# One-token attention decode on one core: all heads but the last summed in one full-width PSUM bank, then carried by an fp32 product into four column groups

## The chip, the cores and the metric

One core of a Trainium2 chip. The time is the device time of one launch, in microseconds. The profile is one execution taken by the hardware profiler; its span (188.0 us) is about 1.8 us shorter than the time reported for the same execution. PE is TensorE, DVE is VectorE, ACT is ScalarE, POOL is GpSimd, SP is the engine that issues the transfers.

## The reference, cut to what matters

```python
x  = A_x                                  # 2 x 1 x 448
xn = layernorm(x)
# attention: 16 query heads on 8 key heads of width 256,
# over the last 4096 positions of two caches
q = xn @ wq
p = softmax(q k^T / 16)
attention = concat_heads(p v) @ wo        # wo: 4096 x 448
dense = mish(xn @ w1 + b1) @ w2           # w2: 1792 x 448
out = x + attention + dense               # 2 x 448
```

The last key window and value window are 4 MB each per key head. All of the output is one sum over contraction blocks of 128 rows: 1 block for x, 14 for the dense part, 4 for each of the 8 key heads.

## The kernel before

The sum lives in PSUM, split into four column groups of 112 of the 448 output columns, each on its own 32 PSUM partitions, so that four matmuls run side by side in the array (16 of them took 0.37 us at 149 us):

```python
NO = NQ                      # 4
DO = D // NO                 # 112
psA = [ps_a.tile([P, DO], FP32, name=f"psA{u}") for u in range(2)]

def part(n):
    return psA[n // 2][n * Q : n * Q + Bsz, :]

def add(lhsT, w, start=False, stop=False):
    for n in range(NO):
        nc.tensor.matmul(part(n), lhsT=lhsT, rhs=w[:, n*DO:(n+1)*DO],
                         start=start, stop=stop, tile_position=(0, n * Q), ...)
```

The loop over key heads is a pipeline: step i scores head i, computes the values of head i-1 and closes head i-2. For the last two heads the values are computed with the cache as the stationary operand, 128 matmuls of 4 columns each:

```python
def values_fixed(i):                       # heads 6 and 7
    state["rec", i] = denominator(i)       # one fp32 matmul, one DVE reciprocal
    ...
    for t in range(T):                     # T = 64
        for c in range(ND):                # ND = 2
            nc.tensor.matmul(po[:, c, :], lhsT=vv[:, t, c, :], rhs=pTv[:, th, 0:Q:HS], ...)
    scale_o(i, po)                         # DVE, writes oT

def mix(kvh):                              # "output matmuls" below: 4 calls of add
    ...
    for h in range(rep):
        for c in range(ND):
            add(oT[:, c, h, :], w[:, h, c * D : (c + 1) * D], stop=...)

for i in range(Hkv + 1):
    ...
    # in step 8, in this order: mix(6), values_fixed(7), scale, mix(7)
```

Head 7's V block arrives in three pieces (positions 0 to 31, 32 to 55, 56 to 63 of 64), so that its values can begin early. The last call of the kernel, `issue_in_order`, makes every engine issue in program order.

The softmax here doesn't subtract the row's maximum and nothing guards it: scores larger than these inputs give would overflow.

Of the kernel before, what the change touches and what calls it, by code (L numbers as in the profile page):

```python
# [12 lines left out]
FP32 = mybir.dt.float32  # L13
# [21 lines left out]
def kernel(  # L35
# [13 lines left out]
    nc = tc.nc  # L49
    P = 128  # L50
    Q = 32
    NQ = P // Q

    Bsz, Sq, D = A_x.shape
    _, Hkv, Sk, Dh = A_k_cache.shape
    HqDh = A_wq.shape[1]
    Hq = HqDh // Dh
    rep = Hq // Hkv
# [14 lines left out]
    ND = Dh // P  # L73
# [9 lines left out]
    ident = lead.tile([P, P], BF16)  # L83
# [5 lines left out]
    consts = ctx.enter_context(tc.tile_pool(name="consts", bufs=1))  # L89
# [5 lines left out]
    ps_a = ctx.enter_context(tc.tile_pool(name="ps_a", bufs=1, space=PSUM))  # L95
# [3 lines left out]
    x_bf = consts.tile([Bsz, D], BF16)  # L99
# [13 lines left out]
    for lo, hi in ((0, SC), (SC, NS)):  # L113
# [4 lines left out]
    ident_f = consts.tile([Q, Q], FP32)  # L118
# [11 lines left out]
        out=rstd[:], in_=mv[:, 1:2], func=ACT.Sqrt, bias=eps_t[:], scale=1.0  # L130
# [5 lines left out]
    for r in range(2):  # L136
        n = (NS + 1 - r) // 2
        nc.vector.tensor_scalar(  # L138
            out=xn_bf[:, r : NS : 2, :, :],
# [12 lines left out]
    for j in range(1, NQ):  # L152
        nc.vector.tensor_tensor(
            out=hsel, in0=hsel, in1=ident[:, j * Q : (j + 1) * Q : HS], op=ALU.add
# [4 lines left out]
    for b in range(Bsz):  # L159
        nc.vector.tensor_reduce(  # L160
            out=off[:, b : b + 1], in_=hsel[:, b * rep : (b + 1) * rep], axis=AXIS.X, op=ALU.add
# [4 lines left out]
        out=off[:], in0=off[:], scalar1=mine[:], scalar2=1e4, op0=ALU.subtract, op1=ALU.mult  # L166
# [12 lines left out]
    for s in range(NS):  # L179
# [7 lines left out]
        out=odd[:],  # L187
        in_=ident[:].rearrange("p (u o) -> p o u", o=2),
# [4 lines left out]
    for par in range(2):  # L193
        for x in range(NX):
            which = (par + x) % 2
            nc.vector.tensor_scalar(
                out=xs[:, par : NS : 2, x, :],
# [6 lines left out]
    nc.vector.memset(ones[:], 1.0)  # L204



    NO = NQ
    DO = D // NO
    psA = [ps_a.tile([P, DO], FP32, name=f"psA{u}") for u in range(2)]  # L210

    def part(n):
        return psA[n // 2][n * Q : n * Q + Bsz, :]

    def add(lhsT, w, start=False, stop=False):
        for n in range(NO):
            nc.tensor.matmul(  # L217
                part(n),
                lhsT=lhsT,
                rhs=w[:, n * DO : (n + 1) * DO],  # L220
                start=start,
                stop=stop,
                tile_position=(0, n * Q),
                skip_group_check=True,
            )

    add(ident[0:Bsz, 0:Bsz], x_bf[:, :], start=True)


    xq = consts.tile([P, NS, NQ, Q], BF16)  # L230
# [102 lines left out]
    def dense_out():  # L333
        w2_sb = dense.pop("w2")
        for x in range(NX):
            for c in range(NF):
                add(act_bf[:, c, x, :], w2_sb[:, x, c, :])
# [13 lines left out]
    def load_k(i, cuts=(0, T)):  # L351
        k_t[i] = k_pool.tile([P, T * Dh], BF16, tag="k", name="k")
        load_cache(k_t[i], A_k_cache, i, cuts)

    def load_v(i, cuts=(0, T)):
        t = v_tile()
        load_cache(t, A_v_cache, i, cuts)
        v_t[i] = t[:].rearrange("p (t d) -> p t d", t=T)

    def load_wo(kvh, parts=1):  # L360
        w = wo_pool.tile([P, rep, ND * D], BF16, tag="wo", name="wo")
        r0 = kvh * rep * Dh
        win = A_wo[r0 : r0 + rep * Dh, :].rearrange("(h p c) d -> p h (c d)", h=rep, p=P)
        for u in range(parts):
            hs = slice(u * rep // parts, (u + 1) * rep // parts)
            nc.sync.dma_start(out=w[:, hs, :], in_=win[:, hs, :])
        wo_t[kvh] = w

    def turn(s):
        kt = kt_pool.tile([P, TH * Dh], BF16, tag="kt", name="kt")  # L370
        i, half = divmod(s, NH)
        k = k_t[i] if half < NH - 1 else k_t.pop(i)
        nc.vector.transpose(  # L373
            out=kt[:].bitcast(FP32),
            in_=k[:, half * TH * Dh : (half + 1) * TH * Dh].bitcast(FP32),
        )
        kt_t[s] = kt

    def scores(s):
        i = s // NH  # L380
        ktv = kt_t.pop(s)[:].rearrange("p (t n c e) -> p n e t c", t=TH, n=NB, e=NE)
        psc = ps_sc.tile([P, TH, Q], FP32, tag="sc", name="sc")
        for n in range(NB):
            for e in range(NE):
                nc.tensor.matmul(  # L385
                    psc[:],
                    lhsT=qdiag[i % NW][:, n * NE + e, :],
                    rhs=ktv[:, n, e, :, :],
                    start=(n == 0 and e == 0),
                    stop=(n == NB - 1 and e == NE - 1),  # L390
                )
        p_sb = p_pool.tile([P, TH * Q], BF16, tag="p", name="p")
        piece = s % NH
        if piece == 0:
            state["rs", i] = small.tile([P, NH, Bsz], FP32, tag="rs", name="rs")
        pv = p_sb[:].rearrange("p (t c b) -> p b t c", t=TH, b=Bsz)
        sv = psc[:].rearrange("p t (c b) -> p b t c", b=Bsz)
        for b in range(Bsz):
            nc.scalar.activation(  # L399
                out=pv[:, b, :, :],  # L400
                in_=sv[:, b, :, :],
                func=ACT.Exp,
                scale=scale,
                bias=off[:, b : b + 1],
                accum_out=state["rs", i][:, piece, b : b + 1],
            )
        p_t[s] = p_sb

    def turn_p(s):
        pT = p_pool.tile([P, TH * Q], BF16, tag="pT", name="pT", bufs=2 * NH + 1)  # L410
        nc.vector.transpose(out=pT[:], in_=p_t.pop(s)[:])  # L411
        pT_t[s] = pT
        i, half = divmod(s, NH)
        if half != NH - 1:
            return
        rs = state.pop(("rs", i))
        total = small.tile([P, 1], FP32, tag="total", name="total")
        nc.vector.tensor_reduce(out=total[:], in_=rs[:], axis=AXIS.XY, op=ALU.add)
        sums = small.tile([P, BR], FP32, tag="sums", name="sums")
        nc.vector.tensor_scalar(  # L420
            out=sums[:], in0=hsel, scalar1=total[:], scalar2=None, op0=ALU.mult
        )
        state["sums", i] = sums
# [45 lines left out]
    def finish(i):  # L469
        ov = state.pop(("o", i))[:].rearrange("r (u m c) -> r u c m", u=NP, c=ND)  # L470
        pq = ps_q.tile([P, NP * ND * NR], FP32, tag="q", name="q")
        pqv = pq[:].rearrange("p (u c r) -> p u c r", u=NP, c=ND)
        for u in range(NP):
            for c in range(ND):
                nc.tensor.transpose(pqv[:, u, c, :], ov[:, u, c, :], ident_f[0:NR, 0:NR])  # L475
        o = small.tile([P, ND, BR], FP32, tag="osum", name="osum")
        nc.vector.tensor_copy(out=o[:], in_=pqv[:, 0, :, 0:BR])
        for u in range(1, NP):
            nc.vector.tensor_tensor(  # L479
                out=o[:], in0=o[:], in1=pqv[:, u, :, u * BR : (u + 1) * BR], op=ALU.add  # L480
            )
        scale_o(i, o)
# [21 lines left out]
    def mix(kvh):  # L504
        oT = state.pop(("oT", kvh))
        w = wo_t.pop(kvh)
        for h in range(rep):
            for c in range(ND):
                add(
                    oT[:, c, h, :],  # L510
                    w[:, h, c * D : (c + 1) * D],
                    stop=(kvh == Hkv - 1 and h == rep - 1 and c == ND - 1),
                )

    NFIX = 2
# [1 line left out]
    def close(i):  # L517
        if i < Hkv - NFIX:
            finish(i)
        mix(i)  # L520
# [7 lines left out]
    for i in range(Hkv + 1):  # L528
        if i + 1 < Hkv:
            load_k(i + 1, (0, T) if i + 1 < Hkv - 1 else (0, T // 2, T))  # L530
        if i < Hkv:
            load_v(i, (0, T) if i < Hkv - 1 else (0, T // 2, 7 * T // 8, T))
            load_wo(i, parts=1 if i < Hkv - 1 else 2)
            for piece in range(NH):
                s = i * NH + piece
                if s + 1 < NSTEP:
                    turn(s + 1)
                scores(s)
                if s >= 1:
                    turn_p(s - 1)  # L540
                if s == NSTEP - 1:
                    turn_p(s)
                if piece == 0 and i > 1:
                    close(i - 2)
            if i + 2 < Hkv:
                build_q(i + 2)
        else:
            close(i - 2)
        if i == 0:
            dense_in()  # L550
            dense_out()
        if i >= 1:
            if i - 1 < Hkv - NFIX:
                values(i - 1)
            else:
                values_fixed(i - 1)
        if i == Hkv:
            close(i - 1)

    res = consts.tile([Bsz, D], BF16)  # L560
    for n in range(NO):
        copy = nc.vector.tensor_copy if n // 2 == 0 else nc.scalar.copy
        copy(out=res[:, n * DO : (n + 1) * DO], in_=part(n))
# [32 lines left out]
```

## Time and profile before

| | |
|---|---|
| time, median of 3 | 190.17 us (189.82 to 190.40) |
| HBM read | 77.67 MB, 413 GB/s over the span |
| busy share of PE, DVE, ACT | 75%, 57%, 23% |
| second piece of the last V block lands | 182.28 us |
| PE idle ahead of that landing | 1.58 us |
| work after that landing to the store | 3.5 us |

Read it from the right: the span is mostly one long stream of transfers, and the end is that stream plus the few steps behind its last landings. What PE does in the stream is free as long as it is ready by then. One more line of this page also belongs here, which the prediction passed over; it counts the transfers that bring the engines' own instructions (queue, kind: packets, MB, share):

```profile
q8 instruction: 8, 0.13, 0.3%
```

Eight transfers, 0.13 MB: 16 KB each.

### The profile page before, as it was taken

What the parts mean: (1) busy time and instruction counts of PE and PEld (TensorE: products, weight loads), DVE (VectorE), ACT (ScalarE), POOL (GpSimd) and SP (SyncE); (2) the same over time, 40 slices, a digit from 0 to 9 for tenths busy, and PEclk for the clock granted to TensorE, in tenths of its full rate; (3) what the DMA queues carried; (4) which work ended last, traced back from release to release, by engine and by line L of the source; (5) the groups of instructions that cost most, each with busy time, mean ns of one, the idle gap of its engine ahead of it and who ended that gap; (6) DMA issues with size and microseconds to landing.
All of it is one profiled execution on the core that took longest, in us unless ns stands there. A gap on an engine that the chain in (4) does not pass through costs nothing.

```text
span 188.0 us, 2587 instructions
## 1 busy us (share of the span) xinstructions
PE 140.3 (75%) x1030; PEld 67.3 (36%) x1030; DVE 106.6 (57%) x141; ACT 42.5 (23%) x142; POOL 16.4 (9%) x74
## 2 busy tenths in 40 slices
PE   0396098905989779966795599956996699988863
PEld 0132033903434334423341334422442334433762
DVE  6604497049931994089704991099506983967201
ACT  3004015200440315012421224021511233134101
POOL 7000600300020001100030003000020000000000
PEclk9999659955999978999999969997899969999855
DMA  6999899999999999999999999999999999999991
GB/s 220 421 476 439 383 426 439 446 443 446 432 439 436 399 404 435 439 439 394 474 441 439 418 404 429 432 446 413 452 446 422 398 425 422 457 439 411 411 385 38
DMA packets 5653, 77.83 MB, mean 414 GB/s; under 512 B 517, under 2 KB 2569, under 8 KB 2954
## 3 DMA queue, kind: packets, MB, share of 16 engines
q1 hardware_dynamic: 5636, 77.66, 97.0%
q8 instruction: 8, 0.13, 0.3%
q10 hardware_dynamic: 6, 0.01, 0.0%
q14 instruction: 3, 0.02, 0.0%
HBM read 77.67 MB, written 0.00 MB: 413 GB/s over the span
## 4 chain that ended last, share of the span: by engine, by line
DMA 67%; DVE 19%; PE 11%; SPq 1%; ACT 1%; issue 0%; ACTq 0%; DVEq 0%
DMA k<-in_A_k_cache_dram 57%; DVE kt L373 14%; DMA v<-in_A_v_cache_dram 10%; PE sc L385 6%; PE o L444 4%; DVE pT L411 3%; PE q L494 1%; ACT p L399 1%; PE psA L217 1%; SPq L114 0%; DVE oT L458 0%; DVE sums L420 0%; SPq L349 0%; DVE osum L479 0%; ACTq L591 0%
## 5 line engine op out<-in xcount | busy, mean ns | idle before, releaser
L373 DVE STREAM_TRANSPOSE kt<-k 128x2048 f32<-128x2048 f32 x32 | 73.1, 2288 | 54.3 <-DMA k<-in_A_k_cache_dram 54.3
L385 PE MATMUL sc<-kt,qdiag 128*128 128x512 bf16 x256 | 68.1, 421 | 19.1 <-DVE kt L373 18.1
L399 ACT ACTIVATE p<-sc,off 128x256 bf16<-128x256 f32 x64 | 33.0, 545 | 72.8 <-PE sc L385 72.1
L385 PEld LDWEIGHTS <-qdiag 128*128 128x128 bf16 x256 | 25.5, 105 | 59.0 <-issue 27.1
L444 PE MATMUL o<-v,pT 128*8 128x512 bf16 x192 | 42.5, 379 | 0.0
L444 PEld LDWEIGHTS <-pT 128*8 128x8 bf16 x192 | 17.2, 92 | 22.4
L266 POOL COPY qdiag<-qt 32x16 bf16<-32x16 bf16 x64 | 13.0, 248 | 120.7 <-PE sc L385 103.8
L411 DVE STREAM_TRANSPOSE pT<-p 128x512 bf16<-128x512 bf16 x32 | 21.5, 673 | 2.5 <-ACT p L399 2.4
L399 ACT ACTIVATION_READ_ACCUMULATOR p<-sc,off 128x1 f32 x64 | 11.8, 184 | 0.0
L452 ACT COPY o_sb<-o 8x512 f32<-8x512 f32 x6 | 3.5, 575 | 36.3 <-PE o L444 36.3
L217 PE MATMUL psA<-wo,oT 128*2 128x112 bf16 x128 | 3.3, 229 | 9.5 <-DVE oT L458 9.5
L246 PE MATMUL q_ps<-v,xq 128*128 128x512 bf16 x28 | 8.8, 491 | 2.0 <-DVE xq L237 2.0
L494 PE MATMUL q<-pT,v 128*128 128x4 bf16 x256 | 7.4, 168 | 2.1 <-DMA v<-in_A_v_cache_dram 1.6
L494 PEld LDWEIGHTS <-v 128*128 128x128 bf16 x256 | 7.4, 101 | 2.3 <-DMA v<-in_A_v_cache_dram 1.7
L217 PE MATMUL psA<-v,act_bf 128*2 128x112 bf16 x56 | 1.5, 296 | 6.5 <-DVE act_bf L331 6.5
L256 DVE CAST q_sb<-q_ps 128x512 bf16<-128x512 f32 x2 | 1.3, 684 | 8.3 <-PE q_ps L246 8.3
L246 PEld LDWEIGHTS <-xq 128*128 128x128 bf16 x28 | 3.3, 121 | 7.2 <-issue 3.5
L217 PEld LDWEIGHTS <-oT 128*2 128x2 bf16 x128 | 1.7, 84 | 10.2 <-DVE oT L458 10.2
L180 PE MATMUL xnT_ps<-ident,xn_bf 2*128 2x2 bf16 x7 | 0.5, 165 | 5.7 <-DVE xn_bf L138 5.7
L458 DVE TENSOR_TENSOR oT<-q,rec 128x8 bf16<-128x8 f32 x2 | 0.3, 166 | 7.0 <-PE q L494 7.0
L475 PEld LDWEIGHTS q<-ident_f,o_sb 8*128 8x128 f32 x24 | 3.3, 207 | 2.6 <-issue 2.6
L475 PE MATMUL q<-ident_f,o_sb 8*128 8x8 f32 x24 | 3.8, 264 | 0.0
(54 smaller groups left out, 43.4 us busy)
## 6 DMA issues: line engine op xcount, KB each, us to landing
k<-in_A_k_cache_dram SPq DMA_DIRECT2D x7, 4096.0 KB, 29.5
v<-in_A_v_cache_dram SPq DMA_DIRECT2D x7, 4096.0 KB, 29.5
k<-in_A_k_cache_dram SPq DMA_DIRECT2D x2, 2048.0 KB, 24.5
v<-in_B_w_dram SPq DMA_DIRECT2D x2, 1568.0 KB, 24.0
wo<-in_A_wo_dram SPq DMA_DIRECT2D x7, 448.0 KB, 30.1
v<-in_A_wq_dram SPq DMA_DIRECT2D x1, 2048.0 KB, 7.5
v<-in_A_v_cache_dram SPq DMA_DIRECT2D x1, 2048.0 KB, 15.1
v<-in_A_wq_dram SPq DMA_DIRECT2D x1, 1536.0 KB, 10.7
```

The lines of the kernel that those rows point to most:

```text
L217: nc.tensor.matmul(part(n), lhsT=lhsT, rhs=w[:, n * DO : (n + 1) * DO], start=start, stop=stop, tile_position=(0, n * Q), skip_group_check ...
L246: nc.tensor.matmul(ps[u][:], lhsT=xq[:, s, :, :].rearrange("p j k -> p (j k)"), rhs=wq_sb[:, s, u * N5 : (u + 1) * N5], start=(s == 0), st ...
L256: copy(out=q_sb[:, u * N5 : (u + 1) * N5], in_=ps[u][:])
L266: nc.gpsimd.tensor_copy(out=tv[rows, :, e, j * Q : (j + 1) * Q : HS].rearrange("p n (b h) -> p n b h", b=Bsz), in_=qv[rows, :, h0 : h0 + r ...
L373: nc.vector.transpose(out=kt[:].bitcast(FP32), in_=k[:, half * TH * Dh : (half + 1) * TH * Dh].bitcast(FP32),)
L385: nc.tensor.matmul(psc[:], lhsT=qdiag[i % NW][:, n * NE + e, :], rhs=ktv[:, n, e, :, :], start=(n == 0 and e == 0), stop=(n == NB - 1 and ...
L399: nc.scalar.activation(out=pv[:, b, :, :], in_=sv[:, b, :, :], func=ACT.Exp, scale=scale, bias=off[:, b : b + 1], accum_out=state["rs", i] ...
L411: nc.vector.transpose(out=pT[:], in_=p_t.pop(s)[:])
L444: nc.tensor.matmul(po[:], lhsT=pT_t[i * NH + piece][:, uh * NP * Q : (uh + 1) * NP * Q : HS], rhs=v[:, u * NP : (u + 1) * NP, :].rearrange ...
L452: nc.scalar.copy(out=o_sb[:], in_=po[:])
L475: nc.tensor.transpose(pqv[:, u, c, :], ov[:, u, c, :], ident_f[0:NR, 0:NR])
L494: nc.tensor.matmul(po[:, c, :], lhsT=vv[:, t, c, :], rhs=pTv[:, th, 0:Q:HS], start=(t == 0 and c == 0), stop=(t == T - 1), skip_group_chec ...
```

## The change

The intent: a full-width sum needs one matmul of 448 columns per block in place of four of 112, so fewer PE instructions. Only the last head, which is closed with nothing left to hide it, keeps the four column groups. What was summed before it is copied to SBUF and put into the groups by four small fp32 products with an identity.

```diff
+    psE = ps_a.tile([Bsz, D], FP32, name="psE")
+    def add(lhsT, w, start=False, stop=False):
+        nc.tensor.matmul(psE[:], lhsT=lhsT, rhs=w, start=start, stop=stop, ...)
+    add(ident[0:Bsz, 0:Bsz], x_bf[:, :], start=True)
-    psA = [ps_a.tile([P, DO], FP32, name=f"psA{u}") for u in range(2)]
+    psA = ps_a.tile([P, DO], FP32, name="psA")
-    def add(lhsT, w, start=False, stop=False):
+    def add_last(lhsT, w, start=False, stop=False):      # the four groups, as before
...
+    def carry():
+        early = consts.tile([Bsz, D], FP32, name="early")
+        nc.vector.tensor_copy(out=early[:], in_=psE[:])
+        add_last(ident_f[0:Bsz, 0:Bsz], early[:, :], start=True)
...                                                      # in mix
+        put = add_last if kvh == Hkv - 1 else add
-                add(
+                put(
...                                                      # in the loop, last step
             close(i - 2)
+            carry()
```

## The prediction

> **What bounds the kernel now.** I read the page's slices first, then the chain of waits, then the timeline of the last 15 us.
>
> ```profile
> PEclk9999659955999978999999969997899969999855
> DMA  6999899999999999999999999999999999999991
> GB/s 220 421 476 439 383 426 439 446 443 446 432 439 436 399 404 435 439 439 394 474 441 439 418 404 429 432 446 413 452 446 422 398 425 422 457 439 411 411 385 38
> ```
>
> Each digit is a fortieth of the span. The transfer engines are busy in every slice but the last, at about 430 GB/s: the caches (77.67 MB read) set the time, and PE (75% busy by the page) has room. The granted PE clock falls to half in the last two slices; remember that for the tail.
>
> ```profile
> DMA 67%; DVE 19%; PE 11%; SPq 1%; ACT 1%; issue 0%; ACTq 0%; DVEq 0%
> ```
>
> The chain of waits says the same. PE steps in the body of it are not thereby on the path: they release transfer issues, and what counts is how much was still queued at each issue. The list of issues gives 29.5 us from issue to landing of a 4096 KB block, and one such block takes some 9.7 us at 430 GB/s, so about three blocks are under way or waiting at all times. Only the end of the chain has no such cushion:
>
> ```profile
> 164.13 18.15 DMA v<-in_A_v_cache_dram
> 182.28 0.05 issue
> 182.33 1.94 PE q L494 x64
> 184.26 0.02 issue
> 184.29 0.18 DVE oT L458
> 184.47 0.04 issue
> 184.51 0.69 PE psA L217 x16
> ```
>
> The second piece of the last V block lands at 182.28; the work that it releases is 64 small matmuls, one DVE scaling, 16 output matmuls, the cast and the store. What PE does just ahead of that landing decides whether the change is felt:
>
> ```profile
> 177.75 0.17 DVE L458 TENSOR_TENSOR oT<-q,rec 128x8 bf16<-128x8 f32 x1 [1.94 <-PE q L494]
> 177.97 0.28 PEld L217 LDWEIGHTS <-oT 128*2 128x2 bf16 x16 [0.35 <-DVE oT L458]
> 177.97 0.54 PE L217 MATMUL psA<-wo,oT 128*2 128x112 bf16 x16 [0.26 <-DVE oT L458]
> 178.45 0.50 PEld L427 LDWEIGHTS den<-sums,ones_f 128*128 128x128 f32 x2 [0.19 <-issue]
> 178.45 0.59 PE L427 MATMUL den<-sums,ones_f 128*128 128x4 f32 x2
> 178.69 1.97 PEld L494 LDWEIGHTS <-v 128*128 128x128 bf16 x64
> 178.90 1.85 PE L494 MATMUL q<-pT,v 128*128 128x4 bf16 x64
> 182.32 1.84 PEld L494 LDWEIGHTS <-v 128*128 128x128 bf16 x64 [1.67 <-DMA v<-in_A_v_cache_dram]
> 182.33 1.93 PE L494 MATMUL q<-pT,v 128*128 128x4 bf16 x64 [1.58 <-DMA v<-in_A_v_cache_dram]
> ```
>
> The column after the start is the length; brackets hold the idle time before. The output matmuls of head 6 (the last but one) start at 177.97, the denominator of head 7 follows, then the first 64 value matmuls; they end at 180.75, and PE is idle 1.58 us until the landing. **That 1.58 us is the whole slack of PE in the tail.** The carry is put between head 6's output matmuls and that denominator.
>
> **What the Trainium skill says.** "TensorE: Matmul & The Clock Gate", Back-to-back issue gap: N/2.4 ns per matmul of N columns at full clock, N/1.2 at half. The trace agrees: around 150.7 to 153.2 us, at a granted 0.50, score matmuls of 512 columns have weight loads 0.43 us apart (512/1.2 = 427 ns). The same page, Part 3 on packing, says that matmuls in different column groups run concurrently and that matmuls start in order; here 16 of 112 columns take 0.37 us at full clock against 16 x 47 = 0.75 us one after the other, so they do overlap. "FP8 and Floating Point Precision", TensorE Precision Notes: true fp32 takes four passes through the array. The trace shows two records per fp32 denominator matmul (16 for 8 heads), which I take as two passes each; with 4 columns they cannot check the rate. "PSUM — Partial Sum Buffer", bank collisions: engines may read one bank together if in different 32-partition quadrants. The final casts now share one bank, DVE in quadrants 0 and 1 and ACT in 2 and 3, so they should still run side by side. No run yet shows it.
>
> **The change part by part.**
> 1. Heads 0 to 5: each head's 16 matmuls of 112 columns become 4 of 448. The old group took 0.37 us, of which 0.30 passed before the next matmul began; the new takes 4 x 448/2.4 = 0.75 us at full clock. That is +0.45 us per head on PE. Instructions fall (the built program has 1739 PE rows instead of 1996), but PE waits for DVE or transfers in every head: before these groups alone it idles 9.5 us in total.
> 2. The dense output: 56 matmuls in 1.48 us become 14 of 448. They start at 44.56 us, where the half-microsecond windows show a clock of 0.50 until about 47.7. 3.2 us at 373 ns is 8.5 of them, the other 5.5 take 187 ns: 4.2 us, +2.8 us. The next V load waits for this (its buffer holds the dense weights): issue at 46.08 moves to about 48.9. But the K block issued at 31.54 lands only at 60.19, so 14 us of transfers are queued ahead. The following scores lose about 1.7 us, DVE some 1 to 2 us, against a DVE idle of 6.83 us before the kt at 60.28. Cost at the end: nothing.
> 3. The last V load is issued at 163.54 when head 5's values are done. From there to 183.6 the windows add up to about 8.2 MB, and that load with its weights is 4.65 MB: 3.6 MB, or 8 us, was still queued. The 0.45 us of part 1 is hidden here too.
> 4. The tail, with all numbers at the half clock granted from 177.4:
>  - head 6: start 177.97; three gaps of 373 ns, 1.12; the last one to its end about 0.57 (a 512-column matmul has 634 ns at most in the trace; 53 less for 64 fewer columns is 0.58). DVE can start at 179.67.
>  - the new DVE copy, 2x448 fp32 out of PSUM: the final 2x112 casts take 265 ns and 128x8 copies 160, so about 1.0 ns for each further element; 0.62 us. With 0.04 to reach PE: 180.33.
>  - the carry: 4 fp32 products of 112 columns, two records each, 2 x 112/1.2 = 187 ns a record. The two records of one group follow each other, and the second of a group overlaps the first of the next (order of start kept), so 5 x 187 = 0.94 us. PE is free at 181.27. All serial would be 1.49, all overlapped about 0.4.
>  - the denominator, 0.45 as now: value matmuls start at 181.72 instead of 178.90.
>  - 128 value matmuls without the wait: 127 x 27.2 ns + 0.17 = 3.6 us, so end at 185.35 instead of 184.26. By then the third V piece (164.78 + 18.8 = 183.6) and the last weights (about 184.0 to 184.6) have landed.
>  - scaling, 16 output matmuls, casts, store: same as now.
> In sum: PE is 2.82 us later at the values, the slack of 1.58 takes most of it, **the end moves by about 1.1 us**. 190.17 + 1.1 = 191.3 us.
>
> **The rivals.**
> - *All of it is hidden* (190.2). It needs the tail to run at full clock: 4 wide matmuls end 0.91 us after their start, copy 0.62, carry 0.5, denominator 0.3, which puts the values at about 180.3 and their first half at 182.1, just ahead of the landing. Speaking for it: 448-column matmuls are denser work than the 4-column ones that let the clock fall. Against: the clock falls at 177.4, before the wide ones begin, and the trace changes clock only at steps of about 3.4 us; the earliest rise would be 180.8. One chance in six.
> - *The carry is dearer* (192): all eight records in sequence, extra weight-load or mode-switch time between the forms. That adds 0.5 to 0.8 us. One chance in six.
> - *A late issue starves the transfers* (192 to 194), through the dense output or the later heads. The backlogs of 14 and 8 us speak against it.
> - *A gain.* PE has fewer instructions and needs fewer fetches; there is a gap of 0.52 us at 176.6 put down to issue. If it goes, head 6 starts 0.5 earlier and the loss halves, but no gain appears: the landing at 182.28 bounds the tail from below.
>
> **Range and chances.** Main line +1.1; half and full overlap of the carry, and the clock, spread it from 0 to +1.9; repeat runs spread by 0.3. Range 190.3 to 192.1. Two per cent is 3.8 us, beyond all but the starving rival, and the transfers exclude a gain of that size.
>
> **What would show it.** Right: the landing of the second V piece stays near 182.3 while no idle "DMA v" stands before the value matmuls any more, and in its place an idle of PE of about 1.2 us between head 6's output matmuls and the carry, released by DVE; the copy takes 0.6 us; the clock stays 0.50. The K and V waits of the body move little and the transfer slices stay at 9. Wrong: idle time for V still before the last value matmuls (then all was hidden), a clock of 1 in the tail, or a V landing that moves by a microsecond or more (then the transfers, not PE, made the change).

## More of the kernel before

All runs with a state were in the fast one. The single looks are of unknown state, as one run alone cannot be judged, and are used for where the time lies, not for small differences of it.

## The result

190.07 us (189.78 to 190.25, 6 runs) against 190.12 us for the kernel before (189.82 to 190.44, 6 runs): ratio 0.9995, interval 0.9979 to 1.001. Ratios here are the mean time of one kernel's fast runs over that of the other's of the same rounds, so not quite the ratio of the medians quoted. **No change; the predicted 191.3 us, and its range from 190.3, were wrong.**

The slices of the changed kernel are of the same kind as before; the chain of waits (start, length, what) ends thus:

```profile
163.86 18.50 DMA v<-in_A_v_cache_dram
182.36 0.04 issue
182.40 1.88 PE q L507 x64
184.29 0.02 issue
184.31 0.18 DVE oT L471
184.49 0.04 issue
184.53 0.69 PE psA L227 x16
```

From the landing on these are, step by step, the last lines of the chain before, within 0.1 us: the landing still bounds the end. The final casts, now out of one tile, run side by side as the prediction expected (DVE from 185.15 for 0.56 us, ACT from 185.21 for 0.52). The timeline just ahead of it shows why (start, length, then in brackets the idle time before):

```profile
173.28 3.52 PE L507 MATMUL q<-pT,v 128*128 128x4 bf16 x128
177.06 1.65 PE L210 MATMUL psE<-wo,oT 128*2 128x448 bf16 x4 [0.26 <-DVE oT L471]
178.75 0.61 DVE L239 COPY early<-psE 2x448 f32<-2x448 f32 x1 [1.74 <-PE psE L210]
179.41 0.55 PE L227 MATMUL psA<-early,ident_f 2*2 2x112 f32 x8 [0.70 <-DVE early L239]
179.89 0.59 PE L440 MATMUL den<-sums,ones_f 128*128 128x4 f32 x2
180.34 1.85 PE L507 MATMUL q<-pT,v 128*128 128x4 bf16 x64
182.40 1.87 PE L507 MATMUL q<-pT,v 128*128 128x4 bf16 x64 [0.22 <-DMA v<-in_A_v_cache_dram]
```

Everything that the prediction put here is here: wide matmuls, a wait for DVE, the copy, the carry. But it starts 0.91 us earlier than head 6's output matmuls did before (177.06, not 177.97), and the carry holds PE for 0.48 us (179.41 to 179.89), not 0.94. So head 7's values start 1.44 us later than before, not 2.82, and the 1.58 us of slack just covers it: 0.22 us of waiting for V is left.

Why does head 6 end earlier? In the kernel before, its 128 value matmuls did not run in one go:

```profile
173.54 3.07 PE L494 MATMUL q<-pT,v 128*128 128x4 bf16 x111
177.13 0.59 PE L494 MATMUL q<-pT,v 128*128 128x4 bf16 x17 [0.52 <-issue]
```

Here 128 take 3.52 us. There the 111th was followed by a hole of 0.52 us that the profile puts down to "issue", that is to no wait that it can see. The bracket counts from the modelled end of the 111th matmul; by start times, which follow each other by 26 ns elsewhere, the hole delays PE by 0.66 us. The rest of the 0.91 us, 0.26, is there before the first value matmul (173.28, not 173.54): in this trace PE had no half-clock spell near 150 us, as it had before from 150.2 to 153.6. The prediction had the hole as a side remark under "A gain". The line on the transfers that bring the engines' own instructions (queue, kind: packets, MB, share) now reads:

```profile
q8 instruction: 7, 0.11, 0.2%
```

One block of 16 KB fewer.

### The profile page after: what moved, and what is told of

Read it like the earlier page. It is cut to its first block, busy times and chain, and to the rows that moved or that the text cites. A ratio compares the mean times of both kernels' runs of the same rounds, so it can differ in the third digit from the quotient of the medians.

```text
span 188.0 us, 2346 instructions
## 1 busy us (share of the span) xinstructions
PE 145.5 (77%) x909; PEld 67.0 (36%) x909; DVE 106.8 (57%) x142; ACT 42.5 (23%) x142; POOL 16.5 (9%) x74
## 4 chain that ended last, share of the span: by engine, by line
DMA 60%; DVE 19%; PE 16%; SPq 2%; ACT 1%; issue 1%; ACTq 0%; DVEq 0%
DMA k<-in_A_k_cache_dram 50%; DVE kt L386 14%; DMA v<-in_A_v_cache_dram 10%; PE o L457 7%; PE sc L398 4%; DVE pT L424 3%; PE psE L210 3%; PE q L507 1%; SPq L362 1%; ACT p L412 1%; SPq L114 0%; PE psA L227 0%; DVE oT L471 0%; PE q L488 0%; SPq L295 0%
## 5 line engine op out<-in xcount | busy, mean ns | idle before, releaser
L386 DVE STREAM_TRANSPOSE kt<-k 128x2048 f32<-128x2048 f32 x32 | 73.1, 2288 | 49.7 <-DMA k<-in_A_k_cache_dram 49.7
L398 PE MATMUL sc<-kt,qdiag 128*128 128x512 bf16 x256 | 63.9, 401 | 17.2 <-DVE kt L386 17.2
L398 PEld LDWEIGHTS <-qdiag 128*128 128x128 bf16 x256 | 24.4, 101 | 56.5 <-issue 23.2
L210 PE MATMUL psE<-wo,oT 128*2 128x448 bf16 x28 | 8.6, 444 | 7.2 <-DVE oT L471 7.2
L210 PE MATMUL psE<-v,act_bf 128*2 128x448 bf16 x14 | 5.2, 567 | 6.5 <-DVE act_bf L344 6.5
L259 PE MATMUL q_ps<-v,xq 128*128 128x512 bf16 x28 | 8.0, 455 | 2.9 <-DMA v<-in_A_wq_dram 2.9
L210 PEld LDWEIGHTS <-act_bf 128*2 128x2 bf16 x14 | 1.6, 121 | 9.5 <-DVE act_bf L344 6.5
L269 ACT CAST q_sb<-q_ps 128x512 bf16<-128x512 f32 x2 | 1.1, 588 | 12.9 <-PE q_ps L259 12.9
```

Of the source, the lines that this page charges most:

```text
L210: nc.tensor.matmul(psE[:], lhsT=lhsT, rhs=w, start=start, stop=stop, skip_group_check=True)
L259: nc.tensor.matmul(ps[u][:], lhsT=xq[:, s, :, :].rearrange("p j k -> p (j k)"), rhs=wq_sb[:, s, u * N5 : (u + 1) * N5], start=(s == 0), st ...
L269: copy(out=q_sb[:, u * N5 : (u + 1) * N5], in_=ps[u][:])
L386: nc.vector.transpose(out=kt[:].bitcast(FP32), in_=k[:, half * TH * Dh : (half + 1) * TH * Dh].bitcast(FP32),)
L398: nc.tensor.matmul(psc[:], lhsT=qdiag[i % NW][:, n * NE + e, :], rhs=ktv[:, n, e, :, :], start=(n == 0 and e == 0), stop=(n == NB - 1 and ...
```

## The experiments

The main theory: the carry costs PE what it seems to cost, and two things paid for it, PE's slack ahead of the V landing and a hole in PE's instruction supply that is gone with the change. The Trainium skill has a place for such a hole: "Runtime: NRT & Kernel Launch", Instruction fetch mechanics, says that each engine's instruction memory is refilled in 16 KiB blocks of 256 instructions, and that the cost of crossing a block border is "mostly hidden". The 16 KB packets agree with the size. The rivals: the hole is chance; the tail of PE does not matter at all, only the transfers do; wide matmuls cost no more than the groups.

### 1 and 2. Both kernels again, for second traces

No edit.

> The kernel before, unchanged, for a second trace. Theory 1 (the 0.67 us hole among head 6's value matmuls at 176.5 us belongs to the kernel: its place is fixed by how many PE instructions come before it, because PE fetches them in blocks): the hole is there again, after the 111th of the 128, within some 10 matmuls. Theory 2 (it is chance of one run): no hole, or one elsewhere, and head 6's output matmuls start 0.6 to 0.9 us earlier, near 177.1. Either way the span stays at 188.0 within 0.5, because the slack before the landing takes it up.

> The changed kernel, unchanged, for a second trace. Theory 1: no hole of over 0.3 us within head 6's value matmuls, head 6's output matmuls again start near 177.1, the carry again takes about 0.5 us, and PE has 0.1 to 0.5 us of idle left before the second V piece lands. Theory 2: any of these can differ by half a microsecond. Span 188.0 within 0.5.

Measured: 190.41 and 190.40 us, spans 188.6 and 188.6, each 0.1 us beyond the 188.5 that was allowed. The kernel before, its timeline and then its chain:

```profile
173.52 3.07 PE L494 MATMUL q<-pT,v 128*128 128x4 bf16 x111
177.67 0.60 PE L494 MATMUL q<-pT,v 128*128 128x4 bf16 x17 [1.08 <-issue]
178.53 0.55 PE L217 MATMUL psA<-wo,oT 128*2 128x112 bf16 x16 [0.26 <-DVE oT L458]
```

```profile
182.33 0.94 PE q L494 x29
183.27 0.60 issue
183.87 1.09 PE q L494 x35
```

The hole is back after exactly the 111th matmul, now 1.08 us long, and a second one stands after the 29th of head 7's second half, that is after its 93rd. **Count the PE instructions between the two holes:** each value matmul is a weight load and a matmul, so 17 x 2 = 34 to the end of head 6, 16 x 2 = 32 output matmuls, 4 records of the fp32 denominator, 93 x 2 = 186: together 256, one block. In the first trace PE reached that second border at 183.12, after its wait for V; the transfer of the block had begun at 180.69, 2.4 us earlier, and no hole shows. The transfer records of the second trace show the two 16 KB blocks beginning at 175.32 and 181.56 us; PE goes on at 177.67 and 183.87, 2.3 us after each. A value matmul starts every 26.4 ns, so 128 pairs use up a block in 3.4 us. No other stretch of this kernel keeps that pace for as long; the next longest are the 56 matmuls of the dense output, 1.48 us.

The changed kernel's second trace has no hole, as expected. **But the same count says that a border is still there:** with 234 instructions fewer ahead of head 6's values, blocks of 256 put it 22 instructions earlier, after the 100th value matmul in place of the 111th. What differs is the transfer. In the changed kernel the last one ahead of that border began at 164.88 and 166.11 us in the two traces, about 11 us before PE got there, and in the kernel before at 174.89 and 175.32, 2.2 to 2.4 us before PE could go on. So the change did not take the border out of the tail, as the expectation of run 5 below has it; the block was asked for early enough. Why it was, no run shows.

The second trace has no slack either: its chain no longer passes through V at the end.

```profile
177.86 0.18 DVE oT L471
178.04 0.04 issue
178.08 1.67 PE psE L210 x4
179.75 0.02 issue
179.78 0.62 DVE early L239
180.40 0.04 issue
180.44 0.55 PE psA L227 x8
180.99 0.52 PE den L440 x2
181.51 3.43 PE q L507 x128
```

Here 128 value matmuls follow each other without a wait, which is the prediction's picture; the 0.1 to 0.5 us of slack that I expected was not there, and head 6's output matmuls start at 178.08, not near 177.1. These two traces can be set against each other stage by stage, since in both PE was at half clock from about 149.9 to 153.3 us:

| stage (start to start on PE) | before | changed | difference |
|---|---|---|---|
| up to the last 8 score matmuls | 171.65 | 172.43 | +0.78 |
| from there to head 6's output matmuls | 6.88 | 5.65 | -1.23 |
| from there to head 7's values (wide sum, copy, carry) | 0.92 | 3.29 | +2.37 |
| head 7's values to their end | 5.50 | 3.56 | -1.94 |
| end of head 7's values | 184.95 | 184.93 | -0.02 |

The first gain is the hole of head 6 (1.08 us by its bracket, 1.22 by start times); the second is the wait for V (1.03 us) and the second hole. The first loss is a thing that the prediction had called hidden: the wider sum of an earlier head (1.12 us in this chain, with a half-clock spell from 149.9, 0.37 before, at 149 us) delays PE, and PE carries that to the tail.

### 3 and 4. More PE work in the tail of either kernel

```diff
         close(i - 2)          # and carry() in the changed kernel
+        fill(4)               # 4 matmuls of 448 columns into a bank nobody reads
```

> The kernel before, with 4 idle-data matmuls of 448 columns (about 1.5 us at half clock) between head 6's output matmuls and head 7's denominator. Theory (PE had 1.58 us of slack there): nothing moves, ratio 0.999 to 1.002. Rival (every microsecond of PE in the tail counts): +1.5 us, ratio 1.008.

> The changed kernel, with the same 4 matmuls at the same place. Theory (the change has used the slack up but for 0.22 us): +1.3 us, about 191.4 us, ratio 1.005 to 1.009. Rival (the end is set by the transfers alone and PE's tail has room in any case, so the change hid nothing): no move, ratio 0.999 to 1.002.

Measured: the kernel before with the filler 189.98 us, ratio 1.0006 (0.9987 to 1.0025); the changed kernel with it 191.68 us, ratio 1.008 (1.0052 to 1.0108). The same filler is free in one and costs its full length in the other: in the profiled run

```profile
179.96 1.58 PE scratch L539 x4
181.54 0.52 PE den L440 x2
182.06 3.43 PE q L507 x128
```

(the chain of the changed kernel with the filler). 191.68 less the 190.07 and 190.16 of the unfilled kernel's sets (other rounds) is 1.5 to 1.6 us. So the rival that PE's tail never counts falls, and so does the one that the change left the slack alone: it used it up. The filler also moved the block border by 8 instructions, and the kernel before shows that in its chain:

```profile
181.10 2.38 PE q L494 x89
183.47 0.14 issue
183.62 1.20 PE q L494 x39
```

89 instead of 93, four pairs earlier, which is 8 instructions, as counted.

### 5. The hole put back into the changed kernel

```diff
             dense_in()
+            pad(117)          # 117 matmuls of 2 columns, in PE's idle before the dense output
             dense_out()
```

> The changed kernel, with 117 tiny matmuls (234 PE instructions, 3 us) put into PE's long idle before the dense output at 38 us, so that the number of PE instructions ahead of head 6's value matmuls is again what it was before the change. Theory (PE fetches its instructions in blocks of 256, and the small value matmuls use them up faster than a block arrives; the change moved the block borders out of the tail): the hole is back after the 111th of head 6's 128 value matmuls, 0.5 to 1.2 us long, a second border stands after the 97th of head 7, and the end moves by +0.5 to +1.0 us, about 190.8 us, ratio 1.002 to 1.006. Rival (the hole was another wait, or chance): no hole at the 111th, ratio 0.999 to 1.001.

Measured: 191.22 us (190.58 to 191.70), ratio 1.0057 (1.0033 to 1.008). The timeline:

```profile
174.26 3.07 PE L507 MATMUL q<-pT,v 128*128 128x4 bf16 x111
178.55 0.60 PE L507 MATMUL q<-pT,v 128*128 128x4 bf16 x17 [1.22 <-issue]
179.41 1.65 PE L210 MATMUL psE<-wo,oT 128*2 128x448 bf16 x4 [0.26 <-DVE oT L471]
```

117 matmuls some 137 us earlier, in time that PE spent idle, bring a hole of 1.22 us back at the very matmul that was named, and 1.0 to 1.2 us to the whole. The padding itself costs nothing where it stands: the dense output starts at 44.63 us and the V block behind it is issued at 50.05 (44.73 and 49.99 without). This is the decisive run: with the borders where they were, the change costs about 1.1 us. That 191.22 is so near the predicted 191.3 is in part luck, as the hole was longer than the one that the prediction's start contained (1.22, not 0.52) and the carry shorter (0.48, not 0.94). The profiled run (191.7 us) is best set beside the second trace of the changed kernel (190.4, one run, so of unknown state), since head 7's last score matmuls start at 172.4 in both: head 6's output matmuls then start 1.33 us later, and the end comes 1.3 us later.

The padding has a hole of its own:

```profile
37.61 2.41 PE L539 MATMUL scratch<-ident 128*2 128x2 bf16 x91
40.27 0.79 PE L539 MATMUL scratch<-ident 128*2 128x2 bf16 x26 [0.25 <-issue]
```

From it to the hole in head 6 the trace has 1258 matmuls and weight loads and 22 semaphore instructions of PE: 1280, five blocks of 256. No hole showed at the second border, after the 97th of head 7; I had expected the border there, and gave no length for it. Its block's transfer began at 182.13 and PE came to it at 185.28, 3.1 us later, so the block had the time that the others lacked.

### 6. The borders of the kernel before moved

```diff
             dense_in()
+            pad(29)
             dense_out()
```

> The kernel before, with 29 such tiny matmuls (58 instructions) at the same early place. Theory: the borders move 29 matmuls forward: the first hole now after the 82nd of head 6, the second after the 64th of head 7, which is just where PE waits for the second V piece, so that it costs nothing. The slow half of the runs of the kernel before (190.3 to 190.4, where its second hole of 0.6 us stood after the landing) should come down to 189.8 to 190.0: ratio 0.997 to 1.000. Rival: holes stay at the 111th and the 93rd, or are gone, ratio 1.000.

Measured: 189.93 us (189.76 to 190.32), ratio 0.9991 (0.9973 to 1.001). The timeline of the profiled run:

```profile
173.87 3.52 PE L494 MATMUL q<-pT,v 128*128 128x4 bf16 x128
178.72 1.87 PE L494 MATMUL q<-pT,v 128*128 128x4 bf16 x64
182.36 1.87 PE L494 MATMUL q<-pT,v 128*128 128x4 bf16 x64 [1.77 <-DMA v<-in_A_v_cache_dram]
```

Both holes are out of sight. The second border fell into the wait for V as planned (its block began at 179.10, so by the 2.3 us seen before PE could go on from 181.4, before the landing). But the hole that I expected after the 82nd of head 6 is not there: that block's transfer began at 164.68 already, in the slow score matmuls. So the place of a border alone does not tell: in these traces it costs something only where PE reaches it less than about 2.3 us after the transfer of its block began. The gain itself lies within the interval: in the kernel before, the slack covered most of its first hole anyway.

### 7 and 8. The carry out of the serial chain

```diff
             close(i - 2)
-            carry()
...                            # in values_fixed
         for t in range(T):
+            if i == Hkv - 1 and t == T // 2:
+                carry()
```

> The changed kernel with the carry moved behind the first half of head 7's value matmuls, where PE waits for V anyway; the DVE copy then runs beside that first half. Theory (the carry sits in the serial chain of the tail and costs 0.7 us of waiting for DVE and 0.5 us of PE there): the first half starts about 1.1 us earlier than in the changed kernel, PE waits for V again by 0.5 us or more, the second half starts at the landing near 182.35: 189.8 to 190.0 us in nearly all runs, ratio 0.997 to 1.000. Rival (the carry was hidden anyhow): the same as the changed kernel, 190.0 to 190.4 in half of the runs.

Measured: 189.88 us (189.72 to 190.07), ratio 0.9985 (0.9966 to 1.0004). Then once more, beside the changed kernel in the same rounds:

> The changed kernel again, on the same chip and in the same rounds as the next one, for their difference. Theory: 190.0 to 190.3 us, runs spread from 189.8 to 190.4 as the half-clock spells of PE fall; ratio to the kernel before 0.998 to 1.002.

> The changed kernel with the carry behind the first half of head 7's value matmuls, again. Theory: 189.8 to 190.0 us with hardly a run above 190.1, 0.1 to 0.3 us below the changed kernel of the same rounds, because no run lacks slack. Rival (chance in the first try): no difference to the changed kernel.

Measured: 190.16 us (189.66 to 190.28), ratio 0.9989 (0.9968 to 1.001) for the changed kernel; 189.87 us (189.67 to 189.93), ratio 0.9977 (0.9957 to 0.9998) with the carry moved. The timeline of the latter:

```profile
177.15 1.65 PE L210 MATMUL psE<-wo,oT 128*2 128x448 bf16 x4 [0.26 <-DVE oT L471]
178.73 0.59 PE L440 MATMUL den<-sums,ones_f 128*128 128x4 f32 x2
179.18 1.85 PE L509 MATMUL q<-pT,v 128*128 128x4 bf16 x64
180.96 0.55 PE L227 MATMUL psA<-early,ident_f 2*2 2x112 f32 x8
182.44 1.87 PE L509 MATMUL q<-pT,v 128*128 128x4 bf16 x64 [0.92 <-DMA v<-in_A_v_cache_dram]
```

Between the wide sum and the values only the denominator is left; the copy runs beside the first 64 value matmuls, the carry (0.55 us) follows them, and PE still waits 0.92 us for V. All 12 timed runs of this version lie between 189.67 and 190.07, while 7 of the 12 of the changed kernel lie above 190.1. Of the two sets of the same rounds alone the means differ by 0.22 us, which is at the edge of their noise; all 24 runs give 0.19 us. It is the best version found, by 0.2% against the kernel before: in its profiled runs the end is the landing plus the same 3.5 us, and no arrangement ahead of the landing can go below that.

### 9. No groups, no carry

```diff
-        put = add_last if kvh == Hkv - 1 else add
+        put = add
...
-            carry()
...
+    nc.vector.tensor_copy(out=res[:], in_=psE[:])   # in place of four casts
```

> No column groups and no carry at all: head 7 too is summed by 4 matmuls of 448 columns into the one bank, and one DVE cast of 2x448 ends it. Theory (after the last landing every PE nanosecond counts): 3 x 373 + 570 = 1.69 us against 0.65 for the 16 narrow ones, cast 0.61 against 0.56: +1.1 us, about 191.1 us, ratio 1.004 to 1.007. Rival (wide matmuls cost no more than four groups, or the end is set by the store): ratio 0.999 to 1.001.

Measured: 190.91 us (190.87 to 191.23), ratio 1.0044 (1.0026 to 1.0062). Its chain:

```profile
184.53 1.67 PE psE L210 x4
186.20 0.02 issue
186.22 0.61 DVE res L575
```

1.67 us against 0.69 for 16 narrow matmuls, and 0.61 for the cast: the sizes expected. So wide sums are not free where nothing hides them, the rival falls, and the reason to keep the groups for the last head holds. Note also the spread: 0.36 us over six runs. Without the carry this kernel has slack and no hole.

### 10 and 11. The late issue of a V block

The wide dense output moved the issue of the second V block from 46.08 to 49.99 us. How much more would the queue bear?

```diff
         for x in range(NX):
+            if x == 1:
+                fill(24)       # or 64
             for c in range(NF):
                 add(act_bf[:, c, x, :], w2_sb[:, x, c, :])
```

> The changed kernel with 24 further matmuls of 448 columns in the middle of the dense output, which delay the issue of the second V block from 50.0 us to some 55 to 59. Theory (a K block issued earlier is under way until about 60.3, so the queue doesn't run dry): no move, ratio 0.998 to 1.002. Rival (a later issue costs what it is late by): +5 us or more, ratio 1.026 or more.

> The same with 64 of them: the issue comes at some 62 to 67 us, after the queue has run dry at about 60.3. Theory: the transfers stand still from about 60.3 until then and all later landings shift by that: +2 to +7 us, ratio 1.01 to 1.035. Rival (the transfers have slack elsewhere): no move.

Measured: with 24 the issue came at 54.38 us, a little before the expected 55 to 59, and the time was 190.26 us, ratio 1.0001 (0.9974 to 1.0029). With 64 it came at 61.31, not 62 to 67, and the time was 195.88 us, ratio 1.0291 (1.0259 to 1.0323). The busy slices of the transfers with 64:

```profile
DMA  6999999998992899999999999999999999999990
```

The dip in slice 13 (58.0 to 62.8 us) is the queue run dry. So 8 us of delay cost nothing and 15 us cost 5 to 6: the cushion that the prediction relied on was there, if some 2 us smaller than the landing at 60.2 made it look: one-microsecond windows show 524 GB/s from 57 to 58 us, 33 from 58 to 59 and nothing from 59 to 62.

## Why the prediction was wrong, by its own steps

- **What bounds the kernel, and the landing:** right. The second V piece lands at 182.36 (182.28 before), and the end follows it.
- **Part 1, the heads:** the size was right (wide sums of 0.92 us to their end in place of 0.37). That it is hidden was right for the transfers and not for PE: under a half-clock spell at 150 us it reached the tail as +0.78. The 1739 and 1996 PE rows of the built programs stand in no profile; the profiles count 1818 and 2060.
- **Part 2, the dense output:** +2.8 us predicted, +3.8 measured (5.24 against 1.48), as the clock rose only at 49.7 in that run, not at 47.7. In the trace of the changed kernel that was taken beside run 8 it rose at 47.2, and the V issue came at 48.64, near the predicted 48.9. Hidden, as said; runs 10 and 11 show the limit.
- **Part 4, head 6's output matmuls:** from their start to the copy 1.70 us predicted, 1.69 measured. The copy: 0.62 and 0.61. The denominator: 0.45 and 0.45.
- **The step that failed: "head 6: start 177.97".** The old start was taken over as if nothing ahead of it would change. It held a hole of the instruction supply, 0.52 us by its bracket and 0.66 by start times (1.08 and 1.22 in the second trace), and the changed kernel has none. The start came at 177.06: 0.65 us of this is the hole, and 0.26 is luck, a half-clock spell near 150 us that this trace does not have. The prediction had the hole, under "A gain", as a chance with half of the loss at stake, and went on without it. To count the borders would not have been enough: the border moved by 11 matmuls only and stayed in the tail, where its block now came early.
- **The second term, the carry:** 0.94 predicted from two records of a group following each other, 0.48 measured, near the "all overlapped about 0.4" that it named. In the trace the first records of the four groups start within 20 ns and the second ones 141 ns after them, so the groups run side by side and not one after another. 0.91 and 0.46 are together the 1.37 us by which 2.82 was too much; what is left, 1.44, is less than the slack of 1.58. By the prediction's own sum (+1.1) the hole alone would have left about +0.4 us, hole and carry together about nothing; these are estimates.
- **The rivals:** "all of it is hidden" came true, but not for its reason. In the profiled run the clock stayed at half through the whole tail, where that rival needed full clock.
- Shown by runs: the hole goes with the number of PE instructions (runs 1, 3, 5), it is worth about 1.1 us in the changed kernel (run 5), the slack is used up (runs 3 and 4), and the carry's place costs about 0.2 us (runs 7 and 8). Open: when exactly a block is asked for, and so why the changed kernel's block came 11 us ahead, which run 6 shows that I cannot yet tell, and what decides the half-clock spells, which fall differently in every trace.

## What to carry to other kernels

When a change removes or adds instructions on an engine that has a stretch of many short ones, look for holes put down to "issue" and count instructions between them; a hole that repeats at the same instruction will move with the count or vanish, depending on how early its block is asked for, so look up when the transfer began; padding or trimming in an idle place is a cheap test for it. Slack ahead of a landing is a budget that several costs share: draw each of them from it in order, and put new serial work (here a copy and a product) behind a wait that is there anyway, not ahead of it. An unchanged total can be two large terms of opposite sign, and it then pays to separate them: here one of the two was a needless cost.

## What the Trainium skill lacked or had wrong

- "Runtime: NRT & Kernel Launch", Instruction fetch mechanics: block and instruction count agree (16 KB packets, 256 instructions between the two holes), but "mostly hidden" misses a case. With value matmuls of 4 columns started every 26.4 ns, two instructions each, a block lasts 3.4 us; PE ran dry for 0.14 to 1.22 us by the brackets, and went on 2.2 to 2.4 us after the block's transfer began. With 3.1 us (run 5) or 11 us (the changed kernel) from there to the border no hole showed. The section says that the next block is fetched while the current one runs, not how far ahead.
- "FP8 and Floating Point Precision", TensorE Precision Notes: it has the four passes of an fp32 matmul, but no page says what they cost in column groups. Four products of 112 columns, eight records, held PE for 0.48 us at half clock; an estimate for one product alone, four passes of 112 columns at the 1.2 columns per ns that the score matmuls show at half clock (512 in 0.43 us), is 0.37 us, so the four groups overlap nearly fully, as bf16 ones do.
